# Moving the rotations and products of one half group for two kernel blocks from the first feed-forward block to the second, and storing kernel rows by kernel block

## The chip, the cores and the metric

The program runs on one core of a Trainium2 chip. The metric is the device time of one execution in microseconds, the median of the runs of a kernel. The engines are TensorE (PE, with its weight loads as PEld), VectorE (DVE), ScalarE (ACT), GpSimd (POOL) and SyncE (SP); POOL and SP issue most of the DMAs, each from a queue of its own that works in order.

## The reference

One layer on 2,048 tokens of 576 channels: an adaptive layer norm, a state-space (S4D) long convolution, a second adaptive layer norm, and a feed-forward network of 4,608 hidden channels with ReLU.

```python
mod = (_silu(c) @ w_mod).reshape(c.shape[0], 6, 1, -1)
sa, ca, ga, sb, cb, gb = (mod[:, i] for i in range(6))
h = layernorm(x) * (1 + ca) + sa
# K[d, l] = 2 Re sum_n C[d, n] exp(A[d, n] dt[d] l);  y = causal convolution of K and h, by FFT
x = x + ga * (conv(h, K) + h * D_skip)
h = layernorm(x) * (1 + cb) + sb
x = x + gb * (relu(h @ w1) @ w2)
```

The kernel K has 576 channels x 2,048 positions. Each value is a sum over 128 states of products of powers of a complex number, and it has to be made on the chip before it can be transformed.

## The kernel before, in words

**Tokens and kernel positions go in four blocks of 512.** The convolution is done blockwise by transforms of length 1,024: the input block s is transformed to a spectrum U, the kernel block s to a spectrum K, and the output block s is a sum of products of spectra (lines 842 to 972, `conv`). Kernel block s is read from the DRAM arrays `kd[s][p]` (p is one of two halves of the channels) by `load_kt`, so the values of kernel block s must be there when `conv(s)` begins.

**The values of the kernel** are made for twelve half groups h of 48 channels. For kernel block 0 that is done at the start of the program. For blocks 1, 2 and 3 it is done by `KGen.rest` (lines 382 to 479), which walks over a list of items `(h, blocks)`. For each item it loads three tables that were kept in DRAM (`load`: W0, Z and W2, 768, 96 and 1,536 KB, issued by POOL); then DVE turns W0 by complex rotations, one for each block of the item (`rot`, lines 403 to 415: two multiplications of 128x1536 and two additions of 128x768); then PE multiplies (`products`, line 440: 192 small matmul records an item, 16 columns for each block of the item); ACT moves the PSUM results to the row tile `ker` in SBUF (line 450, once for each half of an item); and when six half groups of a p are done, POOL stores the rows to `kd` (line 377).

**The feed-forward network is the thread that everything else is tied to.** `ffn` (line 1242) runs 144 groups g, 36 for each token block. A group is `first(g)` (14 matmuls of 512 columns into `hps`, line 1304, then ACT writes `hh` and DVE writes `hl`, the rounded part and the rest of the hidden values) and `second(g)` (14 matmuls into `acc`, line 1329), two groups behind. `hps` has two PSUM buffers, so `first(g)` can't begin before DVE has written `hl(g - 2)`. In token block 0 the weights are also split into a rounded part and a rest, which costs DVE three more instructions a group (`w<-r,w`) and SP two stores; in later blocks the rests are loaded.

**The rest of the work is fed in between.** `step`, called four times a group, draws pieces from a generator of the current token block: block 0 draws `kg.rest` for all twelve half groups and then `conv(1)`; block 1 draws `finish(0)` (adds and stores the output of block 0), `kg.rest` again and then `conv(2)`; block 2 draws `finish(1)` and `conv(3)`; block 3 `finish(2)`. Each piece has a weight, about its DVE time; a step draws while the sum so far is under a target (`rate`: 2.3, 1.85, 1.4 and 0.5 a step in blocks 0 to 3) and while the last four steps have drawn less than 9.0 (block 0) or 7.0. What is still undrawn at the end of a block is drawn then, all at once, since the next block's `first` needs the result (`norm2` writes xs, xh and xl, which `first` reads). The order so written goes through a scheduler that moves instructions a little within each engine's queue; every engine then works through its queue in that order.

In block 0 the list is (0, blocks 1 2 3), (6, block 1), (1, blocks 1 2 3), (7, block 1) and so on up to (5, blocks 1 2 3), (11, block 1): half groups 0 to 5 get all three kernel blocks, half groups 6 to 11 only block 1. Block 1 makes blocks 2 and 3 of half groups 6 to 11. The load of the input block for `conv(1)` (`ahead`, line 830, tile `h`) is tied to come behind the last table load of `rest`.

Of the kernel before, what the change touches and what calls it, by code (L numbers as in the profile page):

```python
# [10 lines left out]
F32 = mybir.dt.float32  # L11
F32R = mybir.dt.float32r
I32 = mybir.dt.int32
AF = mybir.ActivationFunctionType
# [4 lines left out]
P = 128  # L19
# [27 lines left out]
class KGen:  # L47
# [335 lines left out]
    def rest(self, psum, items, beside=iter(())):  # L383


        nc, k = self.nc, self.k
        v = nc.vector.tensor_tensor
        kes, rows = {}, {}
        most = 16 * max(len(blocks) for _, blocks in items)
        with ExitStack() as ctx:  # L390
            pt = k.pool(ctx, f"kr{items[0][1][0]}")
# [35 lines left out]

            def products(h, W1, W2, blocks):
                na = 16 * len(blocks)
                key = (h // 6, blocks)  # L430
                if key not in kes:
                    kes[key] = pt.tile([P, na, 72], F32, name=f"ker_{h}")
                ke = kes[key]
                for half in range(2):
                    ps = psum.tile([P, 6, na], F32, tag="cps", bufs=1, name="kps")
                    for q in range(6):
                        for dd in range(4):
                            ch = dd * 12 + 6 * half + q
                            for r in range(2):
                                nc.tensor.matmul(  # L440
                                    ps[32 * dd : 32 * dd + 32, q, :],
                                    W2[:, r, :, ch],
                                    W1[:, :na, r, ch],
                                    start=(r == 0),
                                    stop=(r == 1),
                                )
                        if q == 2:
                            yield None
                    q0 = 12 * (h % 6) + 6 * half
                    nc.scalar.activation(  # L450
                        ke[:, :, q0 : q0 + 6], ps.rearrange("p q a -> p a q"), AF.Copy
                    )
                    yield None
                rows[key] = rows.get(key, 0) + 1
                if rows[key] == 6:
                    yield -1
                    for i, s in enumerate(blocks):
                        self.store(
                            s, h // 6, ke[:, 16 * i : 16 * i + 16].rearrange("p a q -> p (a q)"),
                            nc.gpsimd,  # L460
                        )

            nxt = load(items[0][0])
            yield -1
# [22 lines left out]
class Body:  # L487
# [198 lines left out]
    def main(self, ctx, kg, first, late):  # L686
        nc, tc, I = self.nc, self.tc, self.I
# [872 lines left out]
```

## Time and profile before

| | us |
|---|---|
| runs: median (lowest to highest of 3) | 1367.7 (1362.72 to 1369.16) |
| the profiled execution | 1365.79 |
| its span, first to last instruction | 1364.0 |
| PE busy / DVE busy / ACT busy / POOL busy in the span | 1230.0 / 871.4 / 503.7 / 193.0 |
| mean granted TensorE clock | 0.952 |

The span can be read as: the making of kernel block 0 and the first convolution (to about 220 us), then the four feed-forward blocks. Their ends can be seen in the rows of ACT's `oT<-acc` and in the transposes `ps_t` of `norm2`: block 0 ends at about 573 us, block 1 at about 856 us, block 2 at about 1117 us. In rows of the profile `kps<-W1r,W2r` are the products of `rest`, `T<-W,Zr` and `W1r<-...` its rotations, `ps_f` and `Z` the forward transforms, `Y` and `T<-K,Ua` the products of spectra, `V` the last butterfly, `ps_i` the inverse transform. A row of a timeline has start, duration, engine, line, operation, names, shapes and count, and in brackets the idle time of the engine before it with what ended it. A row of the stages has, after the stretch and its length, the busy time of PE, PEld, DVE, ACT and POOL (and how many instructions), the granted clock, the share of the 16 DMA engines and GB/s.

### The profile page before, as it was taken

Reading aid. Unit: us, or ns where it says so; the run is one execution under the profiler, and the core shown is the slowest. Engines: PE = TensorE matmul, PEld = TensorE weight load, DVE = VectorE, ACT = ScalarE, POOL = GpSimd, SP = SyncE. Lnnn points to the kernel's source line nnn. Section 1 sums busy time; section 2 is a strip of 40 time slices with the busy share of each in tenths; the row PEclk is TensorE's granted clock in tenths of the full one; section 3 lists DMA queues with packets and bytes.
Section 4 is the critical chain, followed back from the end, with each engine's and each line's share of the span. In section 5 each row is a group of like instructions: output and inputs, shape, how many; then the busy total and the mean of one; then the engine's idle time right before and its main releaser. Section 6 shows DMA issues by size and latency. Waiting matters only on the chain.

```text
span 1364.0 us, 26051 instructions
## 1 busy us (share of the span) xinstructions
PE 1230.0 (90%) x10608; PEld 975.8 (72%) x10608; DVE 871.4 (64%) x1351; ACT 503.7 (37%) x1014; POOL 193.0 (14%) x269
## 2 busy tenths in 40 slices
PE   5124788999999987999999999999999999999998
PEld 3124566778777766777777887777888888888886
DVE  5977978998886699459737986266999222111111
ACT  7986234222223421622234325333322253233321
POOL 1777221111121100021111000100010000000000
PEclk9556789999999998999999999999999999999999
DMA  6666399888798846699689995676997657666651
GB/s 195 243 245 239 123 355 400 288 290 292 257 339 275 321 146 232 203 356 315 241 276 342 300 372 146 207 239 229 324 351 255 184 168 215 201 193 196 198 174 61
DMA packets 132936, 340.47 MB, mean 250 GB/s; under 512 B 22352, under 2 KB 22672, under 8 KB 132816
## 3 DMA queue, kind: packets, MB, share of 16 engines
q1 hardware_dynamic: 106256, 218.36, 49.6%
q0 software_dynamic: 26272, 119.86, 23.8%
q8 instruction: 83, 1.36, 0.4%
q10 hardware_dynamic: 288, 0.59, 0.1%
q14 instruction: 37, 0.30, 0.1%
HBM read 258.55 MB, written 80.22 MB: 248 GB/s over the span
## 4 chain that ended last, share of the span: by engine, by line
PE 66%; DVE 16%; DMA 9%; issue 5%; ACT 2%; POOL 1%; SPq 0%; DVEq 0%; ACTq 0%; POOLq 0%
PE acc L1329 26%; PE hps L1304 26%; PE kps L440 5%; PE ps_f L757 3%; DVE T L509 3%; DVE Y L509 3%; DVE W L509 2%; PE kps L262 2%; DMA Ua<-Ud 2%; DMA Ud<-U 1%; DVE k L133 1%; DMA h<-in_x_dram 1%; DMA Ka<-Rd 1%; PE ps_i L998 1%; DMA W1d<-W 1%
## 5 line engine op out<-in xcount | busy, mean ns | idle before, releaser
L1329 PE MATMUL acc<-hh,w 128*128 128x512 f32 x1296 | 421.9, 400 | 0.3 <-DVE w L509 0.3
L1304 PE MATMUL hps<-xh,w 128*128 128x512 f32 x1152 | 394.3, 401 | 0.8 <-ACT xh L1061 0.8
L1310 DVE SCALAR_TENSOR_TENSOR hl<-hps,hh 128x512 fp32r<-128x512 f32 x144 | 99.1, 688 | 291.4 <-ACT hh L1309 291.1
L1329 PEld LDWEIGHTS acc<-hh,w 128*128 128x128 f32 x1296 | 242.1, 188 | 52.5 <-DVE w L509 0.7
L1329 PE MATMUL acc<-hl,w 128*128 128x512 f32 x720 | 278.9, 399 | 0.0
L1304 PEld LDWEIGHTS hps<-xh,w 128*128 128x128 f32 x1152 | 216.7, 189 | 48.6 <-ACT xh L1061 2.5
L1304 PE MATMUL hps<-xl,w 128*128 128x512 f32 x576 | 230.2, 400 | 0.9 <-DVE xl L1066 0.9
L1309 ACT ACTIVATE hh<-hps 128x512 fp32r<-128x512 f32 x144 | 86.1, 598 | 346.8 <-PE hps L1304 341.5
L1282 ACT ACTIVATE w<-r 128x576 fp32r<-128x576 f32 x144 | 98.7, 686 | 218.4 <-issue 167.3
L1329 PEld LDWEIGHTS acc<-hl,w 128*128 128x128 f32 x720 | 135.4, 188 | 28.2
L1304 PEld LDWEIGHTS hps<-xl,w 128*128 128x128 f32 x576 | 109.1, 189 | 25.6 <-DVE xl L1066 2.4
L1275 ACT ACTIVATE w<-r 128x640 fp32r<-128x640 f32 x142 | 103.9, 732 | 14.6 <-DMA r<-in_w_dram 13.7
L1304 PE MATMUL hps<-xs,w 128*128 128x512 f32 x288 | 97.2, 417 | 12.9 <-DVE hl L1310 12.6
L262 PE MATMUL kps<-W,W 128*32 128x16 f32 x2304 | 40.3, 216 | 75.1 <-POOL W L59 49.7
L262 PEld LDWEIGHTS kps<-W,W 128*32 128x32 f32 x2304 | 37.8, 150 | 79.7 <-POOL W L59 51.0
L440 PEld LDWEIGHTS kps<-W1r,W2r 128*32 128x32 f32 x3456 | 69.0, 146 | 32.3 <-issue 18.6
L440 PE MATMUL kps<-W1r,W2r 128*32 128x48 f32 (+2 forms) x3456 | 78.3, 238 | 8.0 <-issue 4.1
L509 DVE TENSOR_TENSOR Y<-Y,T 128x1152 f32<-128x1152 f32 x64 | 84.7, 1350 | 0.2
L1304 PEld LDWEIGHTS hps<-xs,w 128*128 128x128 f32 x288 | 52.9, 190 | 26.6 <-DVE hl L1310 15.2
L758 ACT ACTIVATE Z<-ps_f 128x288 f32<-128x288 f32 x104 | 42.4, 408 | 63.8 <-PE ps_f L757 63.1
L509 DVE TENSOR_TENSOR w<-r,w 128x512 fp32r<-128x512 f32 (+2 forms) x108 | 58.0, 573 | 8.7 <-ACT w L1282 8.7
L509 DVE TENSOR_TENSOR W<-Z 128x576 f32<-128x576 f32 x52 | 37.1, 754 | 29.7 <-ACT Z L758 29.7
(215 smaller groups left out, 1366.9 us busy)
## 6 DMA issues: line engine op xcount, KB each, us to landing
r<-in_w_dram SPq DMA_DIRECT2D x144, 320.0 KB, 4.2
r<-in_w_dram SPq DMA_DIRECT2D x144, 288.0 KB, 3.7
w<-L1d SPq DMA_DIRECT2D x108, 320.0 KB, 3.1
w<-L2d SPq DMA_DIRECT2D x108, 288.0 KB, 3.2
W2r<-W2d POOLq DMA_DIRECT2D x18, 1536.0 KB, 8.9
W2d<-W SPq DMA_DIRECT2D x12, 1536.0 KB, 7.7
W<-W1d POOLq DMA_DIRECT2D x18, 768.0 KB, 9.0
Ua<-Ud POOLq DMA_DIRECT2D x12, 1152.0 KB, 10.7
```

What stands on the lines that cost most here:

```text
L133: self.nc.vector.scalar_tensor_tensor(f[:, i].rearrange(pair, u=2), th, float(slot), k[:, i].rearrange(pair, u=2), op0=ALU.mult, op1=ALU.s ...
L262: self.nc.tensor.matmul(ps[32 * dd : 32 * dd + 32, 12 * u + q, :], W2[:, r, :, ch], W1[:, u, :, r, ch], start=(r == 0), stop=(r == 1),)
L440: nc.tensor.matmul(ps[32 * dd : 32 * dd + 32, q, :], W2[:, r, :, ch], W1[:, :na, r, ch], start=(r == 0), stop=(r == 1),)
L509: return self.kept(self.nc.vector.tensor_tensor(*args, **kw))
L757: kept(nc.tensor.matmul(o, fc[:, n2, c, :], src(n2), start=True, stop=True))
L758: nc.scalar.activation(Z[:, n2, c], ps[:, :PC], AF.Copy)
L1275: nc.scalar.activation(w[:, 0], r, AF.Copy)
L1282: nc.scalar.activation(w[:, 0:D], r2[g], AF.Copy)
L1304: nc.tensor.matmul(ps, a, x, start=(i == 0), stop=(i == 13))
L1309: nc.scalar.activation(hh, ps, AF.Relu)
L1310: nc.vector.scalar_tensor_tensor(hl, ps, 0.0, hh, op0=ALU.max, op1=ALU.subtract)
L1329: nc.tensor.matmul(acc[i], a, x, start=(f == 0 and j in (0, 3, 6, 9, 12)), stop=(f == NF - 1 and j in (2, 5, 8, 11, 13)),)
```

## The change

Half group 5 is made for kernel block 1 alone in token block 0, and for kernel blocks 2 and 3 in token block 1, as half groups 6 to 11 were already. So `rest` of block 0 has two rotations fewer and its item (5, ...) has products of 16 columns and not 48; `rest` of block 1 has one more item (5, blocks 2 3) at its head: three more table loads, two rotations and 192 matmul records of 32 columns.

Since the rows of a p are now complete at different times for different kernel blocks, the row tiles are kept by kernel block: one for block 1 and one for blocks 2 and 3 together. An item with blocks 1 2 3 takes two ACT instructions for each half, not one. A tile is stored when its last half group of that stage is done. The tile of blocks 2 and 3 for p = 0 goes out in two parts: half groups 0 to 4 in token block 0, four DMAs of 1,024 pieces of 60 values (240 bytes) each; half group 5 in token block 1, four DMAs of 1,024 pieces of 12 values (48 bytes) each. The other stores keep 64 pieces of 4,608 bytes.

```diff
             def products(h, W1, W2, blocks):
                 na = 16 * len(blocks)
-                key = (h // 6, blocks)
-                if key not in kes:
-                    kes[key] = pt.tile([P, na, 72], F32, name=f"ker_{h}")
-                ke = kes[key]
+                p, parts = h // 6, []
+                for part in ((1,), (2, 3)):
+                    if part[0] in blocks:
+                        hs = [x % 6 for x, b in items if x // 6 == p and part[0] in b]
+                        key = p, part
+                        if key not in kes:
+                            kes[key] = pt.tile(
+                                [P, 16 * len(part), 12 * len(hs)], F32, name=f"ker_{h}_{part[0]}"
+                            )
+                        parts.append((key, 16 * blocks.index(part[0]), hs, kes[key]))
...
-                    q0 = 12 * (h % 6) + 6 * half
-                    nc.scalar.activation(
-                        ke[:, :, q0 : q0 + 6], ps.rearrange("p q a -> p a q"), AF.Copy
-                    )
+                    for (_, part), a, hs, ke in parts:
+                        q0 = 12 * (h % 6 - hs[0]) + 6 * half
+                        nc.scalar.activation(
+                            ke[:, :, q0 : q0 + 6],
+                            ps[:, :, a : a + 16 * len(part)].rearrange("p q a -> p a q"), AF.Copy,
+                        )
                     yield None
...
+                for key, a, hs, ke in parts:
+                    if h % 6 < hs[-1]:
+                        continue
                     yield -1
...
+                    for i, s in enumerate(key[1]):
+                        o = self.k.kd[s][p].rearrange("p (a q) -> p a q", q=72)
+                        for t in range(2):
+                            nc.gpsimd.dma_start(
+                                out=o[64 * t : 64 * t + 64, :, 12 * hs[0] : 12 * hs[-1] + 12],
+                                in_=ke[t::2, 16 * i : 16 * i + 16],
+                            )
...
-                [(h + 6 * i, b) for h in range(6) for i, b in enumerate(((1, 2, 3), (1,)))],
+                [
+                    (h + 6 * i, b) for h in range(6)
+                    for i, b in enumerate(((1, 2, 3) if h < 5 else (1,), (1,)))
+                ],
...
-            yield from kg.rest(self.cps, [(h, (2, 3)) for h in range(6, 12)])
+            yield from kg.rest(self.cps, [(h, (2, 3)) for h in range(5, 12)])
```

What the scheduler makes of it shows in the queues. Lines from 427 on stand 11 to 14 lines lower in the changed file (1310 is 1324, 509 is 520, 1304 is 1318, 1329 is 1343, 1049 is 1063, 744 is 758, 748 is 762).

DVE's queue at the end of `rest` in block 0, first before the change. `W_5` and `W_11` are the tables of half groups 5 and 11, `w<-r,w` are splits of weights, and each `hl` closes one feed-forward group:

```order
L408 TENSOR_TENSOR T<-W1r_4653,Zr_4649 128x1536
L410 TENSOR_TENSOR W1r_4653<-W1r_4653,Zr_4649 128x1536
L509 TENSOR_TENSOR w_4867<-r_4658,w_4867 128x64
L412 TENSOR_TENSOR W1r_4653<-W1r_4653,T 128x16x48
L414 TENSOR_TENSOR W1r_4653<-W1r_4653,T 128x16x48
L509 TENSOR_TENSOR w_4867<-r_4658,w_4867 128x512
L509 TENSOR_TENSOR w_4791<-r_4733,w_4791 128x640
L1310 SCALAR_TENSOR_TENSOR hl<-hps,hh 128x512
L408 TENSOR_TENSOR T<-W_11_4882,Zr_4883 128x1536
L410 TENSOR_TENSOR W1r_4903<-W_11_4882,Zr_4883 128x1536
```

And after the change, from the one rotation of half group 5 on:

```order
L408 TENSOR_TENSOR T<-W_5_4683,Zr_4684 128x1536
L410 TENSOR_TENSOR W1r_4688<-W_5_4683,Zr_4684 128x1536
L1324 SCALAR_TENSOR_TENSOR hl<-hps,hh 128x512
L412 TENSOR_TENSOR W1r_4688<-W1r_4688,T 128x16x48
L414 TENSOR_TENSOR W1r_4688<-W1r_4688,T 128x16x48
L520 TENSOR_TENSOR w_4836<-r_4475,w_4836 128x64
L520 TENSOR_TENSOR w_4836<-r_4475,w_4836 128x512
L520 TENSOR_TENSOR w_4728<-r_4658,w_4728 128x640
L1324 SCALAR_TENSOR_TENSOR hl<-hps,hh 128x512
L520 TENSOR_TENSOR w_4988<-r_4660,w_4988 128x64
L520 TENSOR_TENSOR w_4988<-r_4660,w_4988 128x512
L520 TENSOR_TENSOR w_4890<-r_4830,w_4890 128x640
```

The rotation of half group 11 followed that of 5 directly; now the queue holds three feed-forward groups with nothing but splits of weights between the two. The statistics of `h`, the start of `conv(1)`'s own work, stand one group later than before, behind `hl(19)` and no longer around `hl(18)`; the products of spectra, from the second `T<-R,U` on to the last `V`, stand one feed-forward group earlier.

POOL's queue in the middle of `conv(1)`, before. `Ua` is the spectrum of input block 0 that the first product of spectra needs, `Rd` and `Kd` are stores of kernel spectra:

```order
L1237 DMA kt<-kd_1_60 128x16x72
L748 DMA Rd_0_111<-K_0_5563 128x4x576
L748 DMA Kd_0_115<-K_1_0_5615 128x4x576
L744 DMA Ua<-Ud_0_101 128x4x576
L744 DMA R<-Rd_1_110 128x4x576
```

And after:

```order
L1251 DMA kt<-kd_1_60 128x16x72
L758 DMA Ua<-Ud_0_101 128x4x576
L762 DMA Rd_0_111<-K_0_5518 128x4x576
L762 DMA Kd_0_115<-K_1_0_5570 128x4x576
L758 DMA R<-Rd_1_110 128x4x576
```

The load of `Ua` has gone in front of the two stores. Earlier in the same queue the four stores of 240-byte pieces now stand directly behind the W2 load of half group 5 and ahead of the table loads of half group 11 and of the load of `h`; before, all stores of rows stood behind the load of `h`.

PE's queue at the end of block 1, before. `xs_6182` is the input of block 1, `xs_8902` that of block 2, `ps_t` are the transposes of `norm2` that make it, `acc` is `second`:

```order
L1049 MATMUL ps_t<-ident,h_0_8964 128x128 x2
L1049 MATMUL ps_t<-ident,h_1_8965 128x128 x2
L1329 MATMUL acc_36_6519<-hh,w_8845 128x512
L1329 MATMUL acc_36_6519<-hl,w_8845 128x512
L1304 MATMUL hps<-xs_6182,w_8868 128x512 x2
```

These are the last transposes; all of `first(71)` and 14 matmuls of `second` follow before `first(72)` reads `xs_8902`. After the change (the input of block 2 is `xs_9111` there):

```order
L1063 MATMUL ps_t<-ident,h_0_9173 128x128 x2
L1063 MATMUL ps_t<-ident,h_1_9174 128x128 x2
L1343 MATMUL acc_36_6520<-hl,w_9003 128x512
L1343 MATMUL acc_36_6516<-hh,w_9054 128x512 x2
L1343 MATMUL acc_36_6516<-hl,w_9054 128x512
L1318 MATMUL hps<-xs_9111,w_9028 128x512 x2
L1343 MATMUL acc_36_6517<-hh,w_9054 128x512 x2
```

Here only eight of the twenty transposes stand ahead of the first use of `xs_9111`; the others are woven into `first(72)` and `second(71)`.

More of the change, by code (lines that the diff above doesn't have):

```diff
@@ L387, in rest @@
         v = nc.vector.tensor_tensor
-        kes, rows = {}, {}
+        kes = {}
         most = 16 * max(len(blocks) for _, blocks in items)
@@ L448, in products @@
                             yield None
-                    q0 = 12 * (h % 6) + 6 * half
-                    nc.scalar.activation(
-                        ke[:, :, q0 : q0 + 6], ps.rearrange("p q a -> p a q"), AF.Copy
-                    )
+                    for (_, part), a, hs, ke in parts:
[4 more added lines that the diff above has]
+                        )
                     yield None
-                rows[key] = rows.get(key, 0) + 1
-                if rows[key] == 6:
+                for key, a, hs, ke in parts:
+                    if h % 6 < hs[-1]:
+                        continue
                     yield -1
[L457 to L461, printed above, removed]
+                    for i, s in enumerate(key[1]):
[5 more added lines that the diff above has]
+                            )
             nxt = load(items[0][0])
```

## Prediction

> **What bounds the kernel now.** I read the stages first: busy time by engine between the places where the program changes its work.
>
> ```profile
> 240.00:401.00 161.00, 156.47 (x2477) 123.79 (x2479) 145.77 (x153) 37.74 (x69) 21.33 (x32) 0.99 0.83 291
> 401.00:473.00 72.00, 71.02 (x546) 53.31 (x537) 46.83 (x93) 27.76 (x61) 11.97 (x17) 1.00 0.88 306
> 473.00:549.00 76.00, 63.39 (x255) 49.46 (x254) 72.47 (x96) 15.02 (x25) 3.02 (x4) 0.93 0.54 189
> 575.00:614.00 39.00, 36.24 (x303) 28.12 (x305) 21.86 (x25) 10.04 (x18) 8.25 (x13) 0.96 0.98 356
> 614.00:690.00 76.00, 74.94 (x1238) 59.19 (x1235) 61.26 (x73) 20.49 (x41) 11.01 (x16) 1.00 0.82 282
> 690.00:826.00 136.00, 135.45 (x581) 107.16 (x579) 104.71 (x124) 46.00 (x87) 13.66 (x17) 1.00 0.90 315
> ```
>
> Nearly everywhere PE is the busy engine: 156.5 of 161 us while `rest` of block 0 runs, 71.0 of 72 in the first half of `conv(1)`, 74.9 of 76 in `rest` of block 1, 135.4 of 136 in `conv(2)`. One stretch is different: from 473 to 549 us, the products of spectra of `conv(1)`, DVE is busy 72.5 of 76 us and PE only 63.4. Next, what PE waits for in that stretch, and in the rest of block 1 to the first groups of block 2:
>
> ```profile
> PE hps L1304 <- DVE hl L1310: 12.3, 5, 5.0
> ...
> PE kps L440 <- DVE W1r L412: 2.8, 1, 2.8
> PE ps_i L998 <- DVE V L509: 1.7, 1, 1.7
> PE kps L440 <- ACT w L1282: 1.1, 1, 1.1
> ```
>
> So block 0's tail costs 12.3 us of waiting for `hl`, which stands in DVE's queue behind the products; block 1 costs 5.6 us in three waits. Third, the granted clock around the two longest waits:
>
> ```profile
> 526.00:535.00 9.00, 4.04 (x11) 2.94 (x10) 9.00 (x9) 1.31 (x2) 0.00 (x0) 0.66 0.23 76
> 535.00:546.00 11.00, 8.48 (x29) 6.34 (x28) 11.00 (x19) 1.88 (x3) 0.00 (x0) 0.82 0.55 174
> 601.00:609.00 8.00, 5.74 (x109) 4.48 (x110) 5.45 (x6) 1.11 (x3) 1.31 (x2) 0.79 1.03 393
> ```
>
> A wait also slows what follows: 9 x 0.34 + 11 x 0.18 = 5.0 us of clock are missing around the 5.0 us wait and the next one, 8 x 0.21 = 1.7 us around the wait of 2.8. Where PE is fed, a feed-forward group costs twice 3.17 us:
>
> ```profile
> 1323.56 3.17 PE hps L1304 x14
> 1326.73 3.17 PE acc L1329 x14
> ```
>
> **The change, part by part.** The sum is made against the profiled execution, 1365.79 us, which lies 1.9 us under the median of the runs, 1367.7.
>
> *PE.* Rows of small products in block 0 (first two) and block 1, each 1,152 records, six items:
>
> ```profile
> L440 PE MATMUL kps<-W1r,W2r 128*32 128x48 f32 x1152 | 31.2, 266 | 0.7 <-issue 0.7
> L440 PE MATMUL kps<-W1r,W2r 128*32 128x16 f32 x1152 | 24.1, 212 | 3.5 <-issue 3.4
> L440 PE MATMUL kps<-W1r,W2r 128*32 128x32 f32 x1152 | 23.0, 235 | 3.8 <-DVE W1r L412 2.8 <-ACT w L1282 1.1
> ```
>
> An item of 48 columns costs 31.2 / 6 = 5.2 us, of 16 columns 4.0, of 32 columns 3.8. The price hardly falls with the columns, so splitting one item in two nearly doubles it: block 0 gives back 1.2 us, block 1 pays **+3.8 us**, and there PE has no free time to hide it. The 1.2 us are saved ahead of the stretch that DVE bounds, so they don't reach the end; they are not counted.
>
> *DVE.* A rotation is two multiplications and two additions:
>
> ```profile
> L408 DVE TENSOR_TENSOR T<-W,Zr 128x1536 f32<-128x1536 f32 x18 | 31.5, 1751 | 0.0
> L410 DVE TENSOR_TENSOR W1r<-W,Zr 128x1536 f32<-128x1536 f32 x18 | 31.3, 1753 | 13.0 <-PE kps L440 13.0
> L412 DVE TENSOR_TENSOR W1r<-W1r,T 128x768 f32<-128x768 f32 x24 | 22.8, 952 | 0.0
> ```
>
> 2 x 1.75 + 2 x 0.95 = 5.4 us, two of them 10.8 us. They leave a stretch in which DVE already waits for PE (13.0 us at line 410) and where PE is the bound, so by themselves they buy nothing there. The question is whether `conv(1)` begins earlier. Its start hangs on POOL and on a load:
>
> ```profile
> 383.38 0.76 POOL L400 DMA_DIRECT2D W2r<-W2d  x1 [6.11 <-PE kps L440]
> ...
> 385.22 0.77 POOL L835 DMA_DIRECT2D h<-in_x_dram  x1
> 401.50 0.46 DVE L803 BATCH_NORM_STATS2 st<-h 128x6 f32<-128x288 f32 x1 [2.70 <-DMA h<-in_x_dram]
> ```
>
> The gate is the W2 load at 383.38, which waits for PE's products of half group 10; these stand in PE's queue where they stood. So `h` lands at about 401.5 as before and the rotations removed turn into idle time of DVE, as its queue shows with its three groups of bare splits. What does move is the second half: the products of spectra stand one group earlier, and the load of `Ua` stands ahead of two stores.
>
> ```profile
> 452.72 1.16 POOL L1237 DMA_DIRECT2D kt<-kd  x1 [4.87 <-PE ps_f L757]
> ...
> 461.94 0.76 POOL L744 DMA_DIRECT2D Ua<-Ud  x1
> ...
> 466.98 0.83 DVE L509 TENSOR_TENSOR w<-r,w 128x64 fp32r<-128x64 f32 x2 [2.90 <-ACT w L1282]
> 472.85 2.63 DVE L509 TENSOR_TENSOR Y<-K,Ua 128x1152 f32<-128x1152 f32 x2 [5.04 <-issue]
> ```
>
> DVE stood idle 5.0 us before the first product, which came 10.9 us after the issue of `Ua`. Issued right behind `kt`, at 453.9, `Ua` is there at 464.8 and the products begin 8.0 us earlier. The stretch that DVE bounds keeps its length and its work, so it ends 8.0 us earlier, but one feed-forward group that stood before it now stands behind: -8.0 + 6.3 = **-1.7 us** for block 0. One end: the buffer for `Ua` isn't free earlier, and the products begin when the split at 466.98 is done, 5.0 us earlier: +1.3. Other end: DVE's own queue is the limit; with 72 - 46.8 = 25 us idle from 401 to 473 it could be there near 460: -6.5. I take the middle, from the row of the load.
>
> *The end of block 1.* The new item weighs 2 x 5.4 + 4 x 0.7 = 13.6 in the generator, at 1.85 a step 7.4 steps, 1.84 groups, 11.7 us. Everything of `conv(2)` ends that much later in the order. Before, its last instruction and the last use of its result in `first(72)` stood so:
>
> ```profile
> 851.27 0.69 DVE L1066 TENSOR_TENSOR xl<-xf,xh 128x512 fp32r<-128x512 f32 x1 [1.27 <-ACT xh L1061]
> ...
> 858.73 0.39 PE L1304 MATMUL hps<-xl,w 128*128 128x512 f32 x1
> ```
>
> That is 6.8 us to spare; 11.7 later leaves 4.9 us short. Against that, the queue now weaves twelve transposes and `second(71)` into `first(72)`, so PE waits in pieces with work between them. Bounds 0 and 4.9; I take **+2.5 us**, the middle, in pieces too short to cost clock. The 10.8 us of rotations in `rest` of block 1 hide behind PE (DVE has 14.7 us idle from 614 to 690).
>
> *ACT.* Ten halves now take two evacuations:
>
> ```profile
> L450 ACT ACTIVATE ker<-kps 128x288 f32<-128x288 f32 x12 | 5.1, 427 | 41.2 <-PE kps L440 41.2
> L450 ACT ACTIVATE ker<-kps 128x96 f32<-128x96 f32 x12 | 3.1, 256 | 33.6 <-PE kps L440 33.6
> L450 ACT ACTIVATE ker<-kps 128x192 f32<-128x192 f32 x12 | 4.1, 341 | 19.6 <-PE kps L440 19.6
> ```
>
> 0.256 + 0.341 - 0.427 = 0.17 us each, 1.7 us in all. The next half's matmuls wait for them, but three feed-forward matmuls (3 x 3.17 / 14 = 0.7 us) stand between: 0, at most +1.7.
>
> *POOL and DMA.* The loads of `kt` in the DMA view (KB of one and us from issue to landing):
>
> ```profile
> kt<-kd POOLq DMA_DIRECT2D x6, 576.0 KB, 7.7
> ```
>
> And the row of ACT's queue just ahead of which the square roots for `h` stand:
>
> ```profile
> 415.12 0.60 ACT L1309 ACTIVATE hh<-hps 128x512 fp32r<-128x512 f32 x1 [1.76 <-PE hps L1304]
> ```
>
> The nearest row to the small stores is the load of `kt`: 2,048 pieces of 288 bytes, 1.16 us on POOL and 7.7 us to landing. The four stores of 240-byte pieces are 4,096 pieces: about 2.3 us of POOL, in the 6.1 us that it waits before 383.38, and up to 15.4 us of transfer ahead of `h` in POOL's queue. I enter 0, since the statistics of `h` now stand a group later in the order; the case against is a rival. The 48-byte stores and three more loads (2.4 MB, 7 us at 356 GB/s) fall into 575 to 690, where the DMA share is 0.98 and then 0.82: 0, at most +2.8, another wait like the one at the head of `rest`.
>
> Sum: -1.7 + 3.8 + 2.5 = +4.6 us, 1370.4 for an execution like the profiled one and **1372 us** for the median.
>
> **The rivals.** *Block 0's waits go (faster).* If the products meet a DVE without any backlog, the 12.3 us of waiting and the 5.0 us of clock disappear: -17.3 + 3.8 + 2.5 = -11 us, 1357 us; half of it gives 1365. For it: DVE is the bound of just that stretch, and the change takes 10.8 us from DVE in that block. Against it: DVE had 25 us idle before the stretch and still had the wait; the work inside the stretch is the same.
>
> *The second norm of block 1 comes out whole (slower).* `first(72)` waits for the chain from V over transposes to xl without anything woven in: 4.9 us, with the 1.7 us of `ps_i` on V doubled because DVE's queue is fuller, and the clock gone as at 601 to 609, 1.7 us more: 4.9 + 1.7 + 1.7 = 8.3 in place of 2.5, 1378 us. It decides when `xs` comes after the fourteen matmuls that precede it. For it: eight of twenty transposes only stand ahead of the first use. [...]
>
> *Only the costs are real.* `Ua` has to wait for its buffer, the stretch starts late: +1.3 + 3.8 + 2.5 = +7.6, 1375 us.
>
> *Small pieces hold up `h` (slower).* The chain of POOL's queue puts 4,096 pieces before `h`; at twice the 7.7 us of `kt` it lands at 401.5 + 15.4 = 417 and not by 411, where ACT's square roots (ahead of `hh(20)`, 415.12 us) still wait for nothing. Six late, the stretch begins 6 us later: +10.6, 1378 us. [...] No row here shows small stores to DRAM.
>
> **How the numbers follow.** A measurement of this kernel can tell about 0.5%, 6.8 us, from no change: faster is under 1360.9, slower over 1374.5. My forecast has 0.48; with its bounds it reaches from 1365 to 1378 and lies over 1374.5 in a fifth of its cases (0.10). Block 0's waits go: 0.16, nearly all of it faster, 0.15. The second norm whole: 0.14, slower. Only the costs: 0.14, half of it slower. Small pieces: 0.08, slower but 0.03 that land in the free time. Together faster 0.15, slower 0.10 + 0.14 + 0.07 + 0.05 = 0.36, same 0.49. The range takes in the forecast, the costs, the second norm and the upper half of the faster rival: 1360 to 1380.
>
> **What would show it.** Right: the products of `conv(1)` begin near 465 us, PE still waits 9 to 13 us for `hl` in block 0; kps of 32 columns at 27 us and not 23; one to three short waits of PE at `ps_t` or `hps<-xs` at the start of block 2. Wrong: hardly any wait for `hl` (first rival); a wait over 4 us at block 2's start (second); `Ua` issued no earlier than 458 (third); the row of statistics of `h` waiting for its DMA beyond 411 us (fourth).

## The result and the profile after

| | before | after |
|---|---|---|
| median of the runs, us | 1367.7 | 1380.5 |
| lowest to highest of 5 | 1362.0 to 1370.1 | 1374.7 to 1388.1 |
| span of the profiled execution, us | 1364.0 | 1373.0 |
| mean granted clock | 0.952 | 0.945 |

The changed kernel takes 1.0103 times as long, with a 95% interval of 1.0076 to 1.0130: it is slower, by 10 to 18 us. I had forecast 1372 and a range up to 1380. A second set of runs beside other kernels (last in the table of experiments) gave 1.0081 [1.0056, 1.0105]. The profiled execution of after is the shortest of its five, so the two traces differ by 9 us and not by 13.

I cut each trace at the same places of the program: the starts of ACT's `hh` of the feed-forward groups 0, 20, 38 and 73, and the last instruction. Between 0 and 20 lies `rest` of block 0, between 20 and 38 `conv(1)` up to the first groups of block 1, between 38 and 73 the work of block 1, and behind that nothing that the change touches.

| us between the groups | 0 to 20 | 20 to 38 | 38 to 73 | 73 to the end |
|---|---|---|---|---|
| before | 188.6 | 164.7 | 285.9 | 498.2 |
| after | 195.5 | 160.7 | 294.9 | 497.9 |
| difference | +6.9 | -4.0 | +9.0 | -0.3 |

So `conv(1)` gained what I expected in kind, and two stretches lost that I had put down at 0 and at +6.3. What PE waits for in after, from 370 to 580 us and then from 580 to 880:

```profile
PE hps L1318 <- DVE hl L1324: 10.2, 4, 5.0
PE kps L446 <- issue: 7.4, 2, 6.2
...
PE kps L446 <- DVE W1r L412: 2.5, 1, 2.5
PE ps_i L1012 <- DVE x L520: 2.1, 3, 0.9
PE kps L446 <- issue: 2.1, 1, 2.1
PE kps L446 <- ACT w L1296: 1.1, 1, 1.1
PE kps L446 <- DVE W1r L414: 0.5, 1, 0.5
```

The wait for `hl` is still there (12.3 before). What has grown is "issue", a wait for nothing that the profile shows: 0.3 us before in the first of these stretches, 7.4 now, 6.2 of it at once, in the middle of a half of small products. POOL's queue around it:

```profile
371.57 0.77 POOL L400 DMA_DIRECT2D W2r<-W2d  x1 [18.62 <-issue]
372.32 3.29 POOL L469 DMA_DIRECT2D kd<-ker  x4
375.44 0.88 POOL L398 DMA_DIRECT2D W<-W1d  x1
376.15 0.75 POOL L399 DMA_DIRECT2D Zr<-Zd  x1
377.90 0.76 POOL L400 DMA_DIRECT2D W2r<-W2d  x1 [1.01 <-PE kps L446]
379.15 0.53 POOL L848 DMA_DIRECT2D fcU<-in_fcu_dram  x1 [0.48 <-DMA W2r<-W2d]
382.43 0.55 POOL L848 DMA_DIRECT2D fcK<-in_fck_dram  x1 [2.75 <-DMA kd<-ker]
386.01 0.76 POOL L849 DMA_DIRECT2D h<-in_x_dram  x1 [3.04 <-DMA kd<-ker]
```

The four stores of 240-byte pieces go out at 372.3, and POOL then stands twice until one of them is through (2.75 and 3.04 us). PE's row at that place:

```profile
391.60 1.17 PE L446 MATMUL kps<-W1r,W2r 128*32 128x16 f32 x60 [6.16 <-issue]
```

And the stages: the stretch of the stores, the one behind it, and the stretch of products of spectra that the prediction began with (columns as there: busy times, then clock, DMA share, GB/s):

```profile
378.00:391.00 13.00, 7.41 (x151) 5.56 (x151) 1.56 (x3) 0.94 (x2) 2.51 (x4) 0.95 1.05 175
391.00:401.00 10.00, 9.40 (x89) 7.75 (x89) 2.28 (x4) 2.17 (x4) 1.07 (x2) 0.73 1.02 404
...
473.00:549.00 76.00, 65.84 (x267) 52.14 (x266) 70.92 (x104) 16.07 (x26) 3.02 (x4) 0.93 0.55 192
```

For 13 us the DMA engines are full and move 175 GB/s, less than half of the 404 that they reach right after. Then the clock is 0.73 for 10 us, 2.7 us more. The transfers themselves, with KB of one and the median us to landing:

```profile
W2r<-W2d POOLq DMA_DIRECT2D x2, 1536.0 KB, 14.8
h<-in_x_dram POOLq DMA_DIRECT2D x1, 1152.0 KB, 22.6
...
kd<-ker POOLq DMA_DIRECT2D x4, 240.0 KB, 13.8
```

`h` is issued at 386.0 and lands at 408.6. It isn't `h` that is late, though; the statistics wait for DVE's own queue (idle until ACT's `w`, not until a DMA):

```profile
417.08 0.83 DVE L520 TENSOR_TENSOR w<-r,w 128x64 fp32r<-128x64 f32 x2 [6.66 <-ACT w L1296]
417.83 0.81 DVE L817 BATCH_NORM_STATS2 st<-h 128x6 f32<-128x288 f32 x2
```

The small products, and the first product of `conv(1)`, at the time that I had named:

```profile
L446 PE MATMUL kps<-W1r,W2r 128*32 128x16 f32 x1344 | 28.1, 212 | 11.4 <-issue 11.4
L446 PE MATMUL kps<-W1r,W2r 128*32 128x32 f32 x1344 | 26.3, 235 | 6.2 <-DVE W1r L412 2.5 <-issue 2.1 <-ACT w L1296 1.1
L446 PE MATMUL kps<-W1r,W2r 128*32 128x48 f32 x960 | 25.2, 266 | 0.0
```

The first row holds what block 0 lost: 11.4 us of `issue`, where the rows of before have 3.4 (16 columns) and 0.7 (48 columns).

```profile
465.21 2.62 DVE L520 TENSOR_TENSOR T<-K,Ua 128x1152 f32<-128x1152 f32 x2
```

### The profile page after: what moved, and what is told of

The parts are those of the page before. It is cut to its first block, busy times and chain, and to the rows that moved or that the text cites. A ratio compares the mean times of both kernels' runs of the same rounds, so it can differ in the third digit from the quotient of the medians.

```text
span 1373.0 us, 26473 instructions
## 1 busy us (share of the span) xinstructions
PE 1233.9 (90%) x10800; PEld 979.7 (71%) x10800; DVE 871.5 (63%) x1351; ACT 505.8 (37%) x1026; POOL 200.2 (15%) x276
## 3 DMA queue, kind: packets, MB, share of 16 engines
q8 instruction: 84, 1.38, 0.4%
## 4 chain that ended last, share of the span: by engine, by line
PE 72%; DVE 13%; DMA 7%; issue 3%; ACT 2%; POOL 1%; SPq 0%; DVEq 0%; ACTq 0%; POOLq 0%
PE hps L1318 29%; PE acc L1343 29%; PE kps L446 5%; PE ps_f L771 4%; DVE T L520 2%; DVE Y L520 2%; DVE W L520 1%; PE kps L262 1%; DMA Ud<-U 1%; DVE k L133 1%; DMA Zr<-Zd 1%; PE ps_i L1012 1%; DMA Ka<-Rd 1%; DVE W1r L410 1%; DMA W1d<-W 1%
## 5 line engine op out<-in xcount | busy, mean ns | idle before, releaser
L1324 DVE SCALAR_TENSOR_TENSOR hl<-hps,hh 128x512 fp32r<-128x512 f32 x144 | 99.1, 688 | 291.6 <-ACT hh L1323 291.2
L446 PE MATMUL kps<-W1r,W2r 128*32 128x16 f32 (+2 forms) x3648 | 79.6, 235 | 17.7 <-issue 13.5
```

The source lines that it names most:

```text
L446: nc.tensor.matmul(ps[32 * dd : 32 * dd + 32, q, :], W2[:, r, :, ch], W1[:, :na, r, ch], start=(r == 0), stop=(r == 1),)
L1324: nc.vector.scalar_tensor_tensor(hl, ps, 0.0, hh, op0=ALU.max, op1=ALU.subtract)
```

## The experiments

All were timed beside before. The stretches are those of the one profiled execution of each; a single execution can lie some us from its median (most in `rows_ua_last`: span 1372.9, median 1364.0), so verdicts go by the ratio, and stretches serve to see where. Among the five kernels, before one of them, that move no item and store no pieces, 0 to 20 spreads from 188.1 to 191.2.

| kernel | median, us | ratio to before [95%] | 0-20 | 20-38 | 38-73 |
|---|---|---|---|---|---|
| rows_by_block | 1356.3 | 0.9904 [0.9879, 0.9929] | 188.1 | 153.7 | 287.3 |
| rows_ua_first_all | 1356.2 | 0.9917 [0.9886, 0.9948] | 188.5 | 150.3 | 289.0 |
| before_ua_first | 1362.5 | 0.9956 [0.9936, 0.9976] | 189.0 | 157.5 | 287.1 |
| rows_ua_last | 1364.0 | 0.9977 [0.9955, 0.9999] | 191.2 | 161.1 | 290.5 |
| pieces_only | 1363.3 | 0.9960 [0.9937, 0.9983] | 194.2 | 153.2 | 292.4 |
| late_0 | 1368.8 | 1.0003 [0.9982, 1.0024] | 190.3 | 154.6 | 292.6 |
| late_both | 1374.2 | 1.0051 [1.0024, 1.0078] | 190.2 | 156.2 | 296.1 |
| wide | 1376.0 | 1.0061 [1.0037, 1.0084] | 192.4 | 164.3 | 290.2 |
| wide_ua_first | 1367.9 | 0.9986 [0.9966, 1.0006] | 193.3 | 154.3 | 291.2 |
| wide_60 | 1371.6 | 1.0036 [1.0004, 1.0068] | 195.8 | 156.8 | 293.3 |
| wide_48 | 1369.2 | 1.0028 [1.0000, 1.0055] | 198.6 | 151.4 | 292.3 |
| dropped | 1370.2 | 1.0029 [1.0008, 1.0049] | 191.8 | 165.4 | 286.8 |
| dropped_spread | 1365.0 | 0.9968 [0.9941, 0.9995] | 189.2 | 159.7 | 286.8 |
| after_again | 1380.0 | 1.0081 [1.0056, 1.0105] | 197.7 | 160.6 | 293.9 |

The theory after these profiles: small pieces slow all transfers (175 GB/s at full engines), and PE pays (6.2 us). The rivals: the split item alone makes the loss, or the place of the stores in POOL's queue does.

### What makes conv(1) shorter

**rows_by_block** keeps the new code and undoes the move of the half group:

```diff
-                    for i, b in enumerate(((1, 2, 3) if h < 5 else (1,), (1,)))
+                    for i, b in enumerate(((1, 2, 3), (1,)))
...
-            yield from kg.rest(self.cps, [(h, (2, 3)) for h in range(5, 12)])
+            yield from kg.rest(self.cps, [(h, (2, 3)) for h in range(6, 12)])
```

> The items of before with the new evacuations and the stores of whole rows by kernel block: no half group is moved and nothing is stored in pieces. In the order the load of Ua comes ahead of the two stores here too, as in the changed kernel. If the shorter tail of block 0 in the changed kernel (165 us before, 161 after, from group 20 to group 38) comes from that load, this run has it: 1364 us, 3 to 4 us under before. If it comes from the half group that left the block, this run equals before: 1368 us. Neither theory of the loss (small pieces; the split item) expects a loss here: PE waits for nothing around 390 us.

It is 12 us faster than before and beats both kernels. PE's waits from 370 to 580 us, and the stretch of the products:

```profile
PE hps L1315 <- DVE hl L1321: 4.2, 2, 2.8
```

```profile
473.00:549.00 76.00, 71.81 (x304) 57.12 (x303) 72.29 (x116) 20.52 (x36) 3.00 (x4) 0.98 0.64 218
```

DVE is as full as before (72.3 of 76 us), but does 116 instructions there where it did 96, and PE is busy 71.8 us, not 63.4, at a clock of 0.98, not 0.93. (The products begin 8.5 us earlier there, so this stretch also reaches further into what follows them.) The expected 3 to 4 us were far too few. Since this kernel differs from before in the place of `Ua` and in DVE's order, two runs separate the two. **before_ua_first** takes the code of before and holds the two stores behind the load, by an order on POOL's queue alone:

```diff
-                self.save(self.Rd[s][p], K)
+                if s == 1 and p == 0:
+                    saves[p].append((self.Rd[s][p], K))
+                else:
+                    self.save(self.Rd[s][p], K)
...
             nxt = pair(0)
+            for dst, t in saves[p]:
+                self.tc.add_manual_dep(
+                    self.save(dst, t).ins, self.loaded.ins.name,
```

> The kernel before, with the two stores of K of conv(1)'s first half held behind the load of Ua on POOL's queue; DVE's order stays as before but for three products. If the place of that load alone makes the shorter tail of block 0, the stretch from group 20 to group 38 falls from 165 us to about 154 and the time to 1357. If the shorter tail comes from the other order of DVE's queue (more feed-forward groups woven into the products), only part of DVE's idle 5.0 us ahead of the first product goes, and the time is 1364 to 1367.

POOL's queue and PE's waits (370 to 580 us) in that run:

```profile
452.56 0.76 POOL L744 DMA_DIRECT2D Ua<-Ud  x1 [1.48 <-DVE W L509]
455.12 0.76 POOL L748 DMA_DIRECT2D Rd<-K  x1 [1.81 <-DVE K L509]
```

```profile
PE hps L1319 <- DVE hl L1325: 6.2, 2, 3.4
```

`Ua` goes out 9.4 us earlier than in the row of before (452.6 and 461.9), 6.4 of it against group 20, and three of the five waits for `hl` are gone.

**rows_ua_last** does the reverse in rows_by_block, the load behind the last store:

```diff
+            if s == 1 and p == 0:
+                self.tc.add_manual_dep(
+                    self.loaded.ins, self.saved.ins.name,
```

> The run with whole rows by kernel block, with the load of Ua put back behind the two stores; DVE's order stays that of the run with whole rows. If the place of the load alone makes the shorter tail, the gain of that run is lost: about 1367. If DVE's order makes it, most of the gain stays: 1357 to 1361.

Neither theory holds alone. For 20 to 38: 164.7 with neither, 157.5 with the early load, 161.1 with the other order of DVE, 153.7 with both. -7.2 and -3.6 add up to -10.8, and -11.0 is measured. The times go the same way (-6, -3, and -13 us with both). The two act at different ends. Against group 20 the early load brings the first product from 57.7 us to 49.1 (before_ua_first); DVE's other order leaves it at 57.4 (rows_ua_last) but shortens the way from the last instruction of `V` to group 38 from 34.5 to 31.9 us. In DVE's queue the same seven feed-forward groups stand between the first product and the last `V` in all four kernels.

**rows_ua_first_all** is rows_by_block with the edit of before_ua_first without its condition, so that the stores are held behind the load in every convolution and half:

> The run with whole rows, with every store of K in all the convolutions held behind the first load of its product. In block 0 nothing changes against that run but one store; in conv(2) and the second halves the load of Ua or Ka goes 1 to 4 us earlier. Where PE bounds (blocks 1 and 2) an earlier load buys nothing: 1354 to 1357, the run with whole rows. If conv(2)'s end hangs on its loads too, block 1 from group 38 to group 73 falls by 2 to 4 us.

As expected it equals rows_by_block. The 3.4 us that 20 to 38 fell are not in the time.

### What the pieces cost

**pieces_only** is rows_by_block with the rows of blocks 2 and 3 stored in pieces, nothing moved:

```diff
+                        if part == (2, 3) and p == 0:
+                            hs = hs[:5] if h < 5 else hs[5:]
```

> As the run with whole rows, but the kernel rows of blocks 2 and 3 are stored in pieces of 60 values at half group 4 and of 12 values at half group 5; no half group is moved. If the small pieces hold up the other transfers and so PE, PE waits some 4 to 6 us behind the first stores with the clock halved for 3 to 7 us, the traffic falls under 200 GB/s with the DMA engines full, and the time is 5 to 9 us above the run with whole rows (1371 to 1375). If the split item (its second set of 32-column products and the two 16-column items in a row) makes the loss, this run equals the one with whole rows within 2 us.

7 us over rows_by_block (1363.3 and 1356.3, intervals apart), so pieces cost that much without any move. Their place differs too: the 240-byte stores go out at 379.8 us here, the whole rows of rows_by_block at 404.7; wide_ua_first, below, changes the size at one place. The stretch behind the stores, and the wait that came of it:

```profile
383.00:396.00 13.00, 13.00 (x145) 10.44 (x145) 13.00 (x16) 4.23 (x8) 4.01 (x7) 1.00 1.03 189
```

```profile
407.38 0.74 ACT L1288 ACTIVATE w<-r 128x640 fp32r<-128x640 f32 x1 [8.10 <-DMA r<-in_w_dram]
...
409.11 2.32 PE L448 MATMUL kps<-W1r,W2r 128*32 128x48 f32 x96 [4.74 <-ACT ker L459]
```

Again 189 GB/s at full engines. The victim is another one: the feed-forward weights come late, ACT waits 8.1 us for them, and the evacuation of small products that stands behind in ACT's queue makes PE wait 4.7 us.

**late_0** issues the 240-byte pieces after the last products of `rest`, **late_both** the 48-byte pieces of block 1 too:

```diff
+                    if len(hs) == 5:
+                        held.append((key, hs, ke))
+                        continue
```

> The changed kernel with the four stores of 60-value pieces of block 0 issued behind the last products of rest, behind the load of h and the stores of whole rows. If the pieces hold up PE at 390 us, that wait falls from 6.2 us to at most 2 and the time by about 7 us, to 1374, unless the pieces then hold up the load of kt, which would show in the first transforms of conv(1). If two 16-column items in a row starve PE of instructions whatever the traffic, the wait of 4 to 6 us stays and the time is 1380.

> As the run with the 60-value pieces stored late, and the 12-value pieces of block 1 behind block 1's last products as well. If the 48-byte pieces in the middle of block 1's rest hold up W and Zr there, block 1 from group 38 to group 73 falls from 293 us to 288 to 290 and the time from 1369 to 1364 to 1366. If block 1's loss is the split item alone, both stay within 1 us.

late_0 is 11 to 12 us under after, where about 7 were expected. Its wait at the old place is 1.5 us, but there is a second of 2.9 at 405. Half of its gain lies from 20 to 38 (154.6 and 160.7), and there DVE's order differs too: the statistics of `h` stand behind 18 `hl`, in after behind 20.

late_both (`len(hs) in (1, 5)` there) should have gained 3 to 5 us and lost 5 instead. It doesn't test late 48-byte pieces, though: the scheduler moved their stores forward again. The last rows here are the stores of whole rows and `kt`, 80 us behind them:

```profile
615.94 0.56 POOL L399 DMA_DIRECT2D Zr<-Zd  x1 [2.29 <-DVE W1r L410]
616.49 3.28 POOL L475 DMA_DIRECT2D kd<-ker  x4
...
696.42 2.19 POOL L475 DMA_DIRECT2D kd<-ker  x4 [22.06 <-ACT ker L457]
698.55 1.25 POOL L1260 DMA_DIRECT2D kt<-kd  x1
```

In late_0 the same four stores go out at 612.5 us; here they stand behind one more load. wide_60 below tests these pieces by their size.

**wide** stores the two parts in whole rows of two tensors of their own; **wide_ua_first** adds the early `Ua`:

```diff
-                        o = self.k.kd[s][p].rearrange("p (a q) -> p a q", q=72)
+                        o = self.k.kd[s][p] if len(hs) == 6 else self.k.ke[s, hs[0]]
...
-                                out=o[64 * t : 64 * t + 64, :, 12 * hs[0] : 12 * hs[-1] + 12],
-                                in_=ke[t::2, 16 * i : 16 * i + 16],
+                                out=o[64 * t : 64 * t + 64],
+                                in_=ke[t::2, 16 * i : 16 * i + 16].rearrange("p a q -> p (a q)"),
```

> The changed kernel with the parts of block 0 and block 1 in two tensors of their own, stored in whole rows of 3840 and 768 bytes; kt of blocks 2 and 3 is loaded from them by two transfers of 240-byte and 48-byte pieces. The number of bytes stored and the place of the stores are the same. If it is the size of the pieces, both waits (6.2 us at 390, 2.6 us at 638) go, and the time falls by 9 to 12 us to 1369 to 1372, with up to 2 us for the dearer loads of kt. If it is the bytes or the place in POOL's queue, the waits stay and the time is 1378 to 1382. If the split item makes the loss, 1379 to 1381.

> The run with wide rows, with the two stores of K in conv(1)'s first half held behind the load of Ua. The changed kernel with nothing in pieces at the stores and Ua early: the moved half group alone is left. If the parts add up as the stages so far say, conv(1) from group 20 to group 38 falls from 164 us to 157 and the time from 1376 to 1368 or 1369, equal to before: early Ua (-6 us) pays for the narrow items of block 0 and the split item of block 1 (+4 each). If moving the half group frees DVE for more than that, it is under 1362.

wide missed its 1369 to 1372, since the load of `Ua` fell back behind the stores there. 20 to 38 is 164.3 as in before, though the half group has left the block: moving it frees `conv(1)` of nothing. (Against group 20 the first product comes 7.4 us earlier than before, and from the last `V` to group 38 it is 41.1 us in place of 34.5: the group that stood ahead of the products stands behind them.) With `Ua` early the same kernel equals before, and lies 12 us under after. The same bytes, at the same place, in wide_ua_first:

```profile
376.00:391.00 15.00, 12.44 (x392) 10.15 (x394) 4.31 (x8) 2.68 (x6) 4.70 (x8) 1.00 1.00 383
```

```profile
ke<-ker POOLq DMA_DIRECT2D x4, 240.0 KB, 9.0
```

```profile
390.30 1.16 PE L446 MATMUL kps<-W1r,W2r 128*32 128x16 f32 x60 [2.56 <-issue]
```

383 GB/s in place of 175, 9.0 us in place of 13.8, and PE's wait at the same record (60 of a half's 96 remain) 2.6 us in place of 6.2. At this place the size of the pieces does it; the bytes and the place in the queue don't. The stores themselves are dear (13.8 us to landing in 240-byte pieces, 9.0 in whole rows), and the transfers beside them pay too: from issue to landing in after and in wide_ua_first (365 to 420 us), `W` took 18.6 and 11.7 us, `W2r` 14.8 and 11.1, `h` 22.6 and 18.4. Why small pieces are dear, no run shows.

**wide_60** stores only the 48-byte part in pieces; PE, DVE and ACT have the order of wide_ua_first:

```diff
+                        if len(hs) == 1:
+                            o = self.k.kd[s][p].rearrange("p (a q) -> p a q", q=72)
...
+                                    out=o[64 * t : 64 * t + 64, :, 60:72],
+                                    in_=ke[t::2, 16 * i : 16 * i + 16],
```

> The run with wide rows and early Ua, with the 12-value parts of block 1 stored in pieces of 48 bytes at the place and in the shape of the changed kernel; PE, DVE and ACT have the same order as in that run. If the 48-byte pieces hold up the loads of W and Zr in block 1's rest, block 1 from group 38 to group 73 goes from 291 us to 294 or 295 and the time to 1371 or 1372. If they cost nothing, it equals that run within 1.5 us, and the 12 us that the changed kernel lies higher belong to the 60-value pieces and the order that goes with them.

The time rose as the theory of pieces has it, by 0.5% (0.9986 to 1.0036; the intervals still overlap by a hair), the stretch 38 to 73 by 2.1 us; but 0 to 20, in which the two kernels do the same, is also 2.5 us longer in this profile. POOL's queue in block 1, and what DVE waited for from 600 to 650 us:

```profile
611.44 3.27 POOL L470 DMA_DIRECT2D kd<-ker  x4
619.97 0.72 POOL L398 DMA_DIRECT2D W<-W1d  x1 [5.26 <-DVE T L408]
620.67 0.60 POOL L399 DMA_DIRECT2D Zr<-Zd  x1
```

```profile
DVE W1r L410 <- DMA Zr<-Zd: 3.5, 1, 3.5
```

In wide_ua_first `Zr` goes out right behind the stores and this wait doesn't exist. With pieces, the scheduler put `Zr` behind `W`, which has to wait for its buffer. This wait of DVE hardly reaches PE, though. What PE waits for from 580 to 880 us in wide_60:

```profile
PE ps_i L1039 <- DVE x L528: 2.8, 3, 1.3
PE kps L446 <- DVE W1r L412: 2.8, 1, 2.8
PE kps L446 <- issue: 2.6, 2, 1.8
PE kps L446 <- DVE W1r L414: 0.5, 1, 0.5
```

That is 8.7 us, and 6.3 in wide_ua_first, which has no `issue` there. So the profile shows 2.4 us for the 48-byte pieces. The ratios give 0.50%, uncertain by 0.4, and late_0, with the same stores at the same place, lies only 0.17% over wide_ua_first. Whether they cost more than 2 to 3 us is not settled.

**after_again** is the changed kernel beside these:

> The changed kernel once more, unchanged, beside the others on one chip: 1380 us, 0.8 to 1.3% above before; PE waits 4 to 7 us behind the stores of 60-value pieces and block 1 from group 38 to group 73 takes 291 to 295 us.

As expected; the wait behind the stores is 5.7 us.

### What the moved item costs

**dropped** leaves the products of half group 5 for kernel blocks 2 and 3 out of both blocks (half group 4's values stand in their columns), and stores whole rows once:

```diff
-            yield from kg.rest(self.cps, [(h, (2, 3)) for h in range(5, 12)])
+            yield from kg.rest(self.cps, [(h, (2, 3)) for h in range(6, 12)])
...
+                        if len(hs) == 5 and h == 4:
+                            nc.scalar.activation(
+                                ke[:, :, q0 + 12 : q0 + 18],
```

> The changed kernel with the products of half group 5 for kernel blocks 2 and 3 left out altogether (half group 4's values stand in their columns) and whole rows stored once: nothing in pieces, no extra item in block 1. Ua is loaded behind the stores here, as in the run with wide rows, so the run to compare with is that one, 1376. If the moved item costs PE and the end of block 1 what I put down (3.8 + 2.5 us), this run is about 6 us under it, 1370; block 1 from group 38 to group 73 takes 286 us as before. If the loss hangs on the stores alone, it equals the wide run within 2 us. If narrow items next to each other starve PE of instructions, waits of 3 to 4 us of PE for no semaphore stay between 370 and 410 us, since three items of 16 columns follow each other here too.

To compare with wide: 4 us less (1.0029 and 1.0061; 6 expected), and 38 to 73 is 286.8 in place of 290.2. PE's extra records explain it: the row of 32 columns rose from 23.0 to 26.3 us. The wait for no semaphore stayed:

```profile
390.16 1.17 PE L446 MATMUL kps<-W1r,W2r 128*32 128x16 f32 x60 [2.44 <-issue]
```

**dropped_spread** changes the order of its items, **wide_48** multiplies the narrowed item with 48 columns again, 32 of them zeros:

```diff
+                [(h, (1, 2, 3) if h < 5 else (1,)) for h in (0, 6, 1, 7, 2, 8, 5, 3, 9, 4, 10, 11)],
...
+                na = 48 if h == 5 and blocks == (1,) else 16 * len(blocks)
```

> The run that leaves half group 5's products for blocks 2 and 3 out, with the order of the items changed so that at most two items of 16 columns follow each other (half groups 0, 6, 1, 7, 2, 8, 5, 3, 9, 4, 10, 11). If three narrow items in a row drain PE's instructions, the wait of 2.4 us for no semaphore near 390 us goes to at most 1.5 and the stretch from group 15 to group 20 falls from 53 to 50 us, with a shorter such wait (under 1.5) where 8 and 5 meet. If the wait there comes from something else, it stays over 2 us. Its load of Ua comes early, so conv(1) is some 7 us shorter for that reason: about 1361 to 1364 in all.

> The run with wide rows and early Ua, whose narrowed item (half group 5 in block 0) is multiplied with 48 columns again, 32 of them zeros that a memset on DVE wrote: as many instructions, 1.2 us more of PE's work, no rotations more. If narrow items that follow each other drain PE's instructions, the two waits for no semaphore (2.6 us at 390, 1.9 at 408) fall to under 1.5 in sum and block 0 up to group 20 gets 2 to 3 us shorter in spite of the extra work: 1365 to 1366. If the waits come from something else that the moved half group brings, they stay and the time is 1369.

Both miss: a wait of 2.6 us stayed in the one (its stretch 0 to 20 did get shorter, 189.2), 1.0 and 2.3 us in the other, whose stretch got longer. That narrow items next to each other drain PE's instructions has fallen as an account of where these waits stand.

## Why the prediction was wrong

- **What bounds the kernel**: right. DVE bounds the products of `conv(1)` (busy 70.9 of 76 us there in after, PE 65.8), PE nearly all else (busy 133.8 of 138.1 us from 224.03 to 362.16 us, 176.2 of 178.4 from 696.75 to 875.11).
- **PE**: -1.2 and +3.8 put down, -1.2 not to be counted. Measured for block 1: 26.3 - 23.0 = 3.3 us in the row, 3 to 4 us between dropped and wide. Right. Block 0 was put at nothing, and that left out what PE waits for at the small products: `issue` up to group 20 is 4.1 us in before and 8.7 in wide_ua_first, which stores no pieces (11.4 in after). So the moved half group brings 4.6 us of waiting even in whole rows; why, no run shows (wide_48, with 48 columns again, keeps 8.5).
- **DVE, rotations**: right that they buy nothing (164.3 and 165.4 without them, 164.7 with them, `Ua` late in all three).
- **Block 0's tail, -1.7**: the mechanism was right, the size wrong: 20 to 38 fell by 4.0 in after. The first product came at 465.2 as forecast, but by some luck: group 20 stood 4.4 us late (419.5 and 415.1), and against it the product came 12.0 us earlier (45.7 and 57.7), not 8.0. I had priced the early load; that the products also moved up one group, worth 7.4 us of begin in wide, came on top. The charge of one group behind them was right: 41.0 us from the last `V` to group 38 in place of 34.5, +6.5 for my +6.3. With 1.5 us more for the products themselves: -12.0 + 1.5 + 6.5 = -4.0. Where only the load moves and no group changes its place, there is no such charge, and before_ua_first gains 7.2. My rival "block 0's waits go" (1357 us) is what rows_by_block does, 1356: not by the rotations taken away, as I had it, but by load and order.
- **End of block 1, +2.5**: didn't come. After has no wait at `ps_t` or `hps<-xs`; waits at `ps_i` are 2.1 us, 1.7 before.
- **ACT, 0**: right; rows_by_block has twelve split evacuations, two more than after, and none of the other kernels is clearly faster.
- **POOL and DMA, 0**: this is the step that failed. "I enter 0, since the statistics of `h` now stand a group later in the order" looked at one victim, `h`, and found it covered. It is. But 4,096 pieces slow the transfers beside them for 13 us (175 GB/s in after, 383 at that place in wide_ua_first), and the next in need pays: PE's instructions in after, as the packets of their queue have it (PE went on after 6.2 us, 1.1 us behind the end of one), the feed-forward weights in pieces_only (ACT waits 8.1 us). From wide_ua_first (0.9986) to after (1.0081 and 1.0103) the pieces and the order that comes with them cost 13 to 16 us. By stretch, the profile of after_again lies above that of wide_ua_first by 4.4, 6.3 and 2.7 us. In the first is the longer wait, 3.6 us at 391 in after, and the lower clock behind it, about 1 us (0.73 for 10 us, 0.83 in wide_ua_first at the same place). In the last are the 48-byte pieces, "0, at most +2.8": 2.4 us of PE's waits in wide_60. Together that is 7 us, as much as pieces_only lost (there both kinds of pieces go out in block 0). The 6.3 us in the middle aren't shown to come from pieces (see "Open"). My rival "small pieces hold up `h`" (1378 us) had the right cause and the wrong victim; that its time came within 3 us of the measured one is luck.
- **The account**, in ratios: early `Ua` -0.44% (before_ua_first), the moved half group with its other order +0.30% (wide_ua_first), 48-byte pieces +0.50% (wide_60), and what is left, 240-byte pieces with the order of after, +0.45 to +0.67%. These are differences along a chain of runs, so they add up to the measured 0.81 to 1.03% by construction. Each step is uncertain by 0.3 to 0.4%.
- **Open**: why 20 to 38 is 160.7 in after and 154.3 in wide_ua_first. PE waits 10.2 us for `hl` there and 4.9, and the first product stands 4.6 us later against group 20 (45.7 and 41.1). Pieces aren't needed for it: dropped_spread stores none, also loads `Ua` early, and has 159.7 and 46.2. What it shares with after is the place of the statistics of `h` in DVE's queue, behind 20 `hl`, in wide_ua_first behind 19; no run changed that alone. Open too is why PE stops at just that record.

## What to carry to other kernels

A store in small pieces isn't costed by who waits for it, but by what else is in flight (here 175 GB/s in place of 383, and 6.2 us of PE's time): list every transfer that is due in its time, weights and instructions too, and store whole rows, or in a tensor of their own. Where one engine bounds a stretch, look at what stands ahead of its first operand in the DMA queue: one load ahead of two stores was worth 6 us here, more than the change was forecast to cost. When an edit makes the scheduler choose anew, run the edit's parts alone: here rows kept by kernel block, mere bookkeeping, gained 1%, the moved half group took 0.8% of that away again (rows_by_block 0.9904, wide_ua_first 0.9986), and the stores in pieces with their order another 1%.

## What the hardware showed

PE waited at the small products of `rest` for no semaphore 65 times (0.6 us or more) in the sixteen traces, and 60 of these waits ended 1.1 to 1.6 us after a packet of 16,384 bytes on the instruction queue had ended; the other five don't fit. In after such a packet ended at 390.46 and PE went on at 391.60; in wide_ua_first at 388.88 and 390.30. The packet took 1.43 us in after and 0.97 in wide_ua_first; most of the difference is that it began late, 3.6 us after PE had stopped in after and 0.2 us in wide_ua_first (in after_again it took 2.08 us and began 2.1 late). In after the queue moved 84 packets, 1.38 MB. If they were all for PE's 10,800 matmuls and as many weight loads, that is about 64 bytes each, so by this estimate one packet is 256 instructions, and a half of a narrow item (96 matmuls, 96 weight loads) uses up most of one in 1.7 us. In eight of the traces, those with the half group moved or its products dropped, the wait near 390 stood at the same record of a half, with 60 of 96 still to come, and its length went with the traffic: 1.3 to 3.0 us without 240-byte pieces in flight, 5.7 and 6.2 with them. How far ahead of their use PE's instructions are loaded, no run here shows.
